# Placing the swapped values in two operations, later zero fills, wider load spacing, and a new written order in a transformer block on one core

## The chip, the cores and the metric

The kernel runs on one core of a Trainium2 chip. The metric is the device time of one execution in microseconds. Three executions of the kernel before took 259.90, 262.45 and 261.12 us; their median is 261.12 us. One more execution was recorded by the hardware profiler and took 260.01 us, of which the span from the first to the last instruction is 258.3 us.

The engines are named as in the profile: PE is the matrix engine, with its weight loads shown apart as PEld, DVE the vector engine, ACT the scalar engine, POOL the GpSimd engine, SP the engine that here only issues DMA transfers.

## The reference

The reference is a block with two halves on x of 2048 tokens by 512 features: sliding-window attention with 32 heads of 16 features, and an MLP that mixes along the tokens (1792 hidden). Shifts, scales and gates come from a small vector c. Cut to what matters:

```python
def _A_ref(x, wqkv, wo):                 # H = 32, Dh = 16, W = 256
    q, k, v = split(x @ wqkv)
    scores = einsum('bhqd,bhkd->bhqk', q, k) * Dh ** -0.5
    mask = (i - j >= 0) & (i - j < W)
    p = softmax(where(mask, scores, -1e9))
    return einsum('bhqk,bhkd->bhqd', p, v).merge_heads() @ wo
def _B_ref(x, w1, b1, w2, b2):           # mixes over the 2048 tokens
    u = gelu(einsum('bsd,sf->bdf', layernorm(x), w1) + b1)
    return (einsum('bdf,fs->bds', u, w2) + b2).transpose(0, 2, 1)
mod = (silu(c) @ w_mod); sa, ca, ga, sb, cb, gb = parts(mod)
x = x + ga * _A_ref(layernorm(x) * (1 + ca) + sa, wqkv, wo)
x = x + gb * _B_ref(layernorm(x) * (1 + cb) + sb, w1, b1, w2, b2)
```

## The kernel before

The 2048 tokens are worked in four groups G = 0 to 3 of 512. Each group passes through a projection stage (layer norm, transpose, keys, queries, values), an attention stage and a closing stage (output projection, two layer norms). The groups overlap: while attention of group G runs, the projection of G+1 and the closing of G-1 fill the gaps. The attention work is cut into 75 pieces, called chunks 0 to 74 (15, 20, 20 and 20 for the four groups). A chunk is one set of score matmuls into two PSUM tiles (`pss`, three banks, a single buffer; `psb`, one bank, two buffers), two exponentials on ACT that write the tile `et`, one multiplication with the mask on DVE, and value matmuls on PE (`po`), which are called AV here. The exponential of the three banks is the longest ACT operation, so its number (chunk number) serves as a clock in what follows.

Below, operations are named as in the code. For the values of groups 1 to 3 there are four token tiles of 128 each, and each tile passes through this chain: `v` (four matmuls on PE, tile `pv`), `ve` (DVE copies `pv` to `vb`), `vx` (SP issues two transfers of 32 KB, lines 938 and 939, which carry the values of the half that lies on the wrong 64 partitions from `vb` to `vs`), `vp` (POOL places the values in `VT`, four copies of 64x256: from `vb`, `vs`, `vb`, `vs`). `vb` and `vs` have two buffers each, so the `ve` of a tile waits for the `vp` of the tile two before. `VT` has three buffers of 128x4096 which are taken in turn by the groups; outside the blocks that `vp` writes they must hold zeros, which POOL's memsets `z` provide at the start (one of 128x4096 for `VT[1]`, four of 128x1024 for `VT[2]`). `kk` on POOL splits a copied key tile `kb` into `KT` with a mask by parity. `xn` on POOL and `xt` on SP (line 838) normalize a token tile and transpose it by DMA for the next group. `w1l` on SP (line 1028) loads the seven pieces of `w1`, 512 KB each, that the partial sums of the MLP need (`p`, from chunk 52 on); they land in memory that the pool of the modulation weights has released.

PE keeps three spare PSUM banks (`od0` to `od2`) for the tiles of k, q, v, the output projection and the unit sums of AV. A bank comes free when its copy or its multiplication has run.

The order is written out by hand in two tables. `ORDER` (line 60) lists the numbers of all 1129 operations; `run_schedule` (line 154) emits them in that order, and `CHOSEN` (line 114) says which engine takes an operation that has a choice. The wrapper `Ordered` (line 227) holds PE, DVE, ACT and POOL to that order, and every instruction that it issues has its line, L235. SP is not wrapped (`dma = nc.sync`, line 220): the queue of SP is laid out by the tile framework when the program is built, so it need not follow `ORDER`. In the built program of the kernel before, SP holds, from the fourth transpose for group 2 on: three loads of w1, the fourth `vx` of group 1, four loads of w1, all four transposes for group 3, and then the first `vx` of group 2.

After the attention stage PE alone sets the pace: partial sums, first MLP layer (`u`, `pu`), and second layer (`py`), until 16 tiles of output have been stored.

Of the kernel before, what the change touches and what calls it, by code (L numbers as in the profile page):

```python
# [17 lines left out]
DH = 16  # L18
# [42 lines left out]
    2, 38, 0, 4, 9, 40, 3, 10, 11, 12, 41, 13, 6, 14, 8, 42, 39, 16, 5, 43, 44, 45, 46, 17, 48, 18, 19, 47, 1, 20,  # L61
    52, 51, 50, 7, 49, 56, 57, 58, 60, 59, 61, 53, 74, 62, 75, 126, 76, 79, 127, 77, 63, 84, 80, 55, 64, 85, 78,
    128, 130, 81, 65, 83, 82, 89, 131, 86, 93, 67, 54, 66, 90, 129, 88, 134, 132, 87, 71, 91, 72, 135, 73, 68, 92,
    69, 94, 70, 136, 138, 95, 97, 139, 98, 264, 96, 110, 99, 140, 265, 142, 111, 143, 101, 100, 106, 266, 112, 144,
    166, 267, 102, 113, 167, 145, 103, 268, 15, 104, 168, 170, 107, 171, 141, 146, 114, 137, 147, 115, 148, 133,
    172, 174, 116, 108, 149, 175, 269, 117, 151, 150, 152, 490, 156, 271, 153, 184, 176, 119, 173, 118, 154, 120,
    272, 185, 121, 491, 273, 157, 155, 270, 122, 158, 105, 188, 169, 186, 27, 124, 189, 28, 274, 492, 161, 29, 275,
    162, 159, 125, 198, 163, 24, 160, 123, 190, 276, 493, 25, 199, 21, 177, 109, 22, 26, 200, 202, 23, 30, 164, 494,
    203, 165, 178, 278, 179, 180, 187, 204, 206, 191, 31, 181, 207, 277, 192, 193, 32, 194, 37, 182, 495, 216, 208,
    279, 183, 201, 217, 280, 209, 286, 281, 287, 195, 220, 218, 282, 283, 288, 221, 284, 36, 289, 291, 219, 285,  # L70
    292, 496, 497, 222, 205, 328, 196, 296, 329, 293, 297, 34, 210, 716, 290, 294, 330, 332, 197, 211, 333, 331,
    212, 223, 301, 302, 499, 298, 213, 336, 334, 35, 306, 295, 299, 214, 33, 337, 307, 215, 717, 500, 224, 225, 308,
    338, 346, 501, 498, 718, 310, 347, 311, 339, 309, 226, 944, 502, 303, 348, 350, 312, 227, 230, 351, 300, 335,
    945, 233, 234, 719, 228, 360, 352, 231, 229, 235, 361, 304, 720, 313, 314, 353, 239, 362, 315, 364, 240, 365,
    232, 236, 504, 340, 241, 366, 368, 305, 237, 369, 242, 946, 317, 341, 243, 342, 370, 238, 378, 316, 343, 318,
    379, 349, 320, 319, 321, 244, 721, 344, 354, 380, 382, 345, 355, 383, 245, 324, 503, 325, 246, 384, 392, 322,
    356, 393, 371, 512, 326, 513, 357, 367, 396, 394, 509, 514, 397, 510, 363, 247, 515, 511, 372, 398, 723, 400,
    947, 381, 505, 358, 248, 401, 506, 249, 385, 373, 725, 374, 359, 327, 402, 410, 507, 517, 375, 323, 411, 395,
    518, 386, 387, 519, 376, 414, 250, 727, 412, 532, 415, 533, 377, 516, 728, 388, 403, 255, 416, 424, 522, 520,
    389, 399, 425, 523, 251, 534, 417, 508, 426, 428, 524, 404, 390, 429, 256, 405, 525, 539, 391, 521, 413, 406,  # L80
    724, 430, 252, 432, 540, 407, 433, 431, 527, 722, 253, 528, 541, 427, 434, 535, 442, 536, 408, 435, 443, 537,
    409, 529, 418, 542, 444, 254, 446, 530, 543, 447, 257, 419, 948, 526, 420, 538, 448, 554, 258, 544, 421, 555,
    449, 436, 726, 437, 545, 259, 438, 556, 445, 558, 546, 439, 557, 422, 547, 559, 423, 729, 450, 451, 548, 440,
    562, 560, 452, 441, 949, 261, 563, 459, 561, 460, 263, 730, 456, 564, 461, 572, 262, 453, 457, 565, 573, 731,
    531, 458, 732, 454, 468, 576, 574, 550, 455, 577, 549, 733, 462, 463, 469, 578, 950, 586, 464, 465, 587, 260,
    466, 470, 551, 467, 588, 590, 553, 735, 591, 471, 736, 552, 566, 472, 737, 592, 594, 567, 589, 595, 579, 738,
    748, 593, 596, 604, 749, 605, 597, 739, 473, 575, 568, 750, 569, 608, 606, 740, 475, 580, 581, 570, 607, 741,
    609, 582, 474, 598, 951, 571, 477, 476, 583, 618, 610, 752, 619, 481, 479, 753, 599, 478, 751, 584, 622, 754,
    620, 600, 585, 623, 755, 482, 743, 734, 756, 480, 624, 626, 744, 611, 601, 627, 483, 742, 745, 628, 636, 484,
    746, 612, 637, 613, 757, 485, 614, 621, 602, 640, 638, 762, 603, 625, 641, 772, 763, 629, 773, 615, 764, 650,  # L90
    642, 774, 488, 651, 765, 759, 760, 643, 486, 630, 639, 616, 761, 654, 487, 652, 631, 655, 632, 653, 644, 489,
    617, 645, 646, 747, 633, 658, 656, 952, 634, 657, 953, 659, 954, 635, 957, 660, 668, 958, 647, 661, 669, 955,
    959, 956, 960, 670, 672, 662, 648, 673, 649, 663, 671, 664, 961, 767, 674, 780, 963, 665, 675, 781, 964, 768,
    965, 782, 769, 784, 966, 666, 770, 785, 667, 676, 783, 677, 967, 678, 786, 788, 685, 679, 787, 789, 686, 682,
    771, 687, 683, 680, 798, 790, 776, 681, 684, 799, 688, 758, 791, 689, 777, 694, 800, 802, 691, 779, 778, 803,
    766, 692, 695, 968, 693, 804, 812, 969, 801, 813, 805, 775, 792, 690, 793, 794, 814, 696, 816, 795, 970, 817,
    697, 974, 971, 698, 975, 818, 972, 820, 796, 976, 821, 815, 973, 806, 819, 807, 797, 808, 822, 830, 809, 977,
    823, 831, 979, 699, 978, 980, 981, 832, 701, 700, 834, 810, 824, 835, 811, 825, 703, 702, 826, 982, 707, 836,
    704, 844, 985, 983, 845, 986, 837, 987, 833, 988, 827, 846, 848, 990, 705, 989, 849, 991, 708, 992, 993, 709,
    850, 852, 828, 838, 853, 829, 839, 994, 840, 1001, 706, 995, 854, 862, 841, 1002, 710, 863, 996, 984, 847, 711,  # L100
    997, 855, 998, 864, 851, 866, 962, 842, 1003, 867, 843, 999, 911, 1000, 912, 868, 876, 908, 913, 877, 714, 909,
    865, 1007, 713, 910, 1004, 878, 880, 712, 856, 1005, 881, 857, 914, 715, 858, 1008, 869, 882, 884, 859, 1012,
    883, 885, 1009, 915, 1013, 1010, 879, 860, 894, 916, 861, 1014, 895, 917, 1018, 1011, 1019, 919, 870, 886, 918,
    871, 896, 898, 1015, 897, 899, 887, 1020, 1021, 1016, 872, 900, 888, 1022, 901, 1030, 1017, 889, 873, 920, 890,
    874, 902, 891, 903, 1006, 875, 892, 904, 893, 1059, 905, 921, 1038, 906, 1073, 907, 1039, 922, 926, 927, 923,
    929, 928, 1031, 930, 932, 1032, 1052, 931, 1023, 925, 1024, 933, 1053, 1045, 924, 934, 1066, 1025, 935, 1046,
    936, 1026, 1074, 937, 1027, 939, 1067, 1047, 1028, 938, 1075, 1060, 1040, 940, 1029, 1033, 1080, 941, 1081, 943,
    1054, 942, 1061, 1082, 1034, 1041, 1035, 1048, 1062, 1042, 1036, 1076, 1049, 1043, 1055, 1087, 1056, 1050, 1068,
    1088, 1063, 1069, 1037, 1089, 1044, 1108, 1057, 1070, 1101, 1064, 1051, 1083, 1058, 1102, 1077, 1071, 1094,
    1095, 1065, 1078, 1084, 1090, 1103, 1085, 1091, 1109, 1096, 1097, 1122, 1098, 1104, 1115, 1105, 1110, 1072,  # L110
    1111, 1086, 1092, 1116, 1079, 1123, 1099, 1112, 1117, 1118, 1106, 1100, 1124, 1093, 1125, 1119, 1113, 1107,
    1120, 1126, 1114, 1127, 1121, 1128,
]
CHOSEN = {
    "ACT": [
        47, 48, 51, 76, 78, 88, 1022, 1027,
    ],
    "DVE": [
        49, 50, 52, 70, 73, 81, 83, 86, 91, 95, 99, 101, 104, 108, 112, 114, 117, 119, 122, 124, 248, 250, 252, 254,
        277, 278, 281, 285, 288, 293, 298, 303, 308, 312, 315, 319, 322, 326, 474, 476, 478, 480, 503, 504, 507, 511,  # L120
        514, 519, 524, 529, 534, 538, 541, 545, 548, 552, 700, 702, 706, 729, 730, 733, 737, 740, 745, 750, 754, 757,
        761, 764, 769, 774, 778, 956, 961, 967, 972, 978, 983, 989, 994, 1000, 1005, 1011, 1016,
    ],
    "POOL": [
        704,
    ],
}
BATCH = True
XT_AFTER = -0.7
W1_AFTER = 2.0  # L130
AV_POS = 0.2
LZ_POS = 0.0
M_POS = -0.5
OT_POS = -1.0
# [59 lines left out]
def kernel(  # L194
# [243 lines left out]
    box = {}  # L438
# [17 lines left out]
    def e_stps(e):  # L456
# [8 lines left out]
            deps=[o3], pos=-20)  # L465
# [142 lines left out]
    def proj0():  # L608
# [3 lines left out]
        def normed(half):  # L612
# [43 lines left out]
            if half == 0:  # L656
# [4 lines left out]
                               deps=[cp[dc // 2], o_fm], pos=base + 1.5) for dc in range(ND)]  # L661
                transposed.setdefault(0, []).append(z)
                zeros[2] = [
                    op("z", "POOL", 0.87, lambda e, n=n: po.memset(VT[2][:, 2 * n : 2 * n + 2, :, :], 0.0), deps=hs[half], pos=base + 3.0)
                    for n in range(4)
                ]
            else:
# [684 lines left out]
```

## Time and profile before

| what | value |
|---|---|
| median of three executions | 261.12 us (259.90 to 262.45) |
| profiled execution | 260.01 us, span 258.3 us, mean granted PE clock 0.993 |
| PE busy, share of the span | 236.3 us, 91% |
| DVE, ACT, POOL busy | 203.2, 179.3, 128.1 us |
| first exponential of chunk 0 | 12.57 us after the start |
| last exponential of chunk 74 begins | 174.35 us |
| last stretch, PE alone | about 176 to 255 us |

The busy shares are averages over stages with different limits. Between 20 and 175 us ACT is the fullest engine; after that ACT has little to do and PE has no gaps. So the time is read in two stretches: how early ACT gets through its exponentials, and how much work is then left for PE.

### The profile page before, as it was taken

The numbers are of one execution on the slowest core, as the hardware profiler recorded it, in microseconds if no ns is written. First come the engines' busy times: TensorE is split into PE (matmuls) and PEld (weight loads), VectorE is DVE, ScalarE is ACT, GpSimd is POOL, SyncE is SP. The second block draws the span as 40 slices with busy tenths as digits, with TensorE's granted clock in tenths as the row PEclk, the third lists the DMA queues.
The fourth block names the chain that finished last, engine by engine and source line by source line (L and its number), as shares of the span: only waits on it lengthen the run. The fifth ranks groups of instructions, "written<-read, shape, count | busy, mean of one in ns | idle before, by whom it ended". The sixth has DMA issues, their size and how long they took to land.

```text
span 258.3 us, 8085 instructions
## 1 busy us (share of the span) xinstructions
PE 236.3 (91%) x3385; PEld 122.0 (47%) x3427; DVE 203.2 (79%) x394; ACT 179.3 (69%) x255; POOL 128.1 (50%) x235
## 2 busy tenths in 40 slices
PE   7878889899895999987999999999999999999994
PEld 2555554444442453444544454446444444444443
DVE  5689999998996999899668889898868764444443
ACT  4499999999996999999999999997237410000000
POOL 8587995975994989787904793810000000000000
PEclk9999999999998899999999999999999999999999
DMA  6998421369923000000020024024999201111111
GB/s 220 328 350 244 38 53 25 61 165 288 182 43 51 13 7 1 3 14 13 15 81 13 4 84 139 28 84 130 374 324 394 84 22 42 46 58 41 41 43 41
DMA packets 41341, 27.02 MB, mean 105 GB/s; under 512 B 11992, under 2 KB 37208, under 8 KB 41304
## 3 DMA queue, kind: packets, MB, share of 16 engines
q1 hardware_dynamic: 41008, 25.97, 35.7%
q8 instruction: 27, 0.44, 0.7%
q10 hardware_dynamic: 296, 0.53, 0.6%
q14 instruction: 10, 0.08, 0.1%
HBM read 22.03 MB, written 2.10 MB: 93 GB/s over the span
## 4 chain that ended last, share of the span: by engine, by line
PE 59%; ACT 18%; DVE 15%; issue 5%; DMA 1%; SPq 0%; DVEq 0%
PE py L235 18%; PE pu L235 17%; ACT et L235 15%; PE pss L235 8%; PE po L235 7%; DVE et L235 4%; PE pa L235 3%; DVE vb L235 2%; DVE h L235 2%; ACT lz L235 2%; PE pk L235 2%; PE pv L235 2%; DVE QT L235 1%; DVE st L235 1%; DVE kb L235 1%
## 5 line engine op out<-in xcount | busy, mean ns | idle before, releaser
L235 ACT ACTIVATE et<-pss 128x1536 bf16<-128x1536 f32 x75 | 110.9, 1478 | 2.5 <-PE psb L235 1.8
L235 PE MATMUL pu<-hb,w1p 128*128 128x512 bf16 x213 | 50.8, 380 | 1.2 <-issue 0.9
L235 DVE TENSOR_TENSOR et<-et,maskt 128x1024 bf16<-128x1024 bf16 (+2 forms) x79 | 47.0, 616 | 5.5 <-ACT et L235 5.4
L235 PE MATMUL py<-guT,w2r 128*128 128x512 bf16 (+1 forms) x234 | 48.5, 366 | 0.7 <-DVE otile L235 0.5
L235 ACT ACTIVATE et<-psb 128x512 bf16<-128x512 f32 x75 | 47.0, 628 | 0.0
L235 PE MATMUL pss<-QT,KT 32*128 32x64 bf16 (+3 forms) x720 | 30.1, 232 | 7.2 <-ACT et L235 5.5
L235 PEld LDWEIGHTS <-w2r 128*128 128x128 bf16 x238 | 23.3, 98 | 26.0 <-issue 0.7
L235 PE MATMUL po<-et,VT 128*32 128x64 bf16 (+3 forms) x960 | 32.3, 235 | 1.8 <-DVE vb L235 0.4
L235 PEld LDWEIGHTS <-w1p 128*128 128x128 bf16 x224 | 20.3, 98 | 25.1 <-issue 2.4
L235 PE MATMUL po<-et,ones_bd 128*32 128x256 bf16 (+3 forms) x624 | 31.5, 269 | 0.0
L235 DVE TENSOR_TENSOR otile<-py,xr 128x512 bf16<-128x512 f32 (+1 forms) x17 | 11.2, 660 | 25.5 <-PE py L235 25.3
L235 PEld LDWEIGHTS <-KT 32*128 32x128 bf16 x960 | 16.4, 93 | 29.0 <-issue 27.0
L235 POOL TENSOR_SCALAR KT<-kb,mask_par 128x512 bf16<-128x512 bf16 (+1 forms) x38 | 26.2, 701 | 7.0 <-DVE kb L235 3.9
L235 PE MATMUL psb<-QT,KT 32*128 32x64 bf16 (+3 forms) x240 | 29.5, 232 | 0.0
L235 PEld LDWEIGHTS <-VT 128*32 128x32 bf16 x960 | 19.0, 96 | 15.4 <-issue 13.1
L235 POOL TENSOR_SCALAR xn<-x,rs,nm 128x512 bf16<-128x512 bf16 x24 | 23.5, 984 | 2.2 <-DVE h L235 1.2
L235 PE MATMUL pk<-h1T,wqkv 128*128 128x256 bf16 (+2 forms) x102 | 20.5, 322 | 3.3 <-DVE vb L235 2.4
L235 DVE BATCH_NORM_STATS2 st<-x 128x6 f32<-128x512 bf16 x32 | 21.7, 684 | 1.5 <-DMA x<-in_A_x_dram 1.3
L235 PEld LDWEIGHTS <-wqkv 128*128 128x128 bf16 x164 | 13.8, 97 | 15.7 <-issue 7.6
L235 PE MATMUL pv<-wqkv,h1T 128*64 128x256 bf16 (+1 forms) x107 | 16.9, 320 | 0.2
L235 PE MATMUL pa<-wod,OT 128*128 128x512 bf16 x58 | 16.0, 380 | 0.5 <-issue 0.3
L235 POOL COPY VT<-vb 64x256 bf16<-64x256 bf16 x24 | 12.8, 535 | 7.1 <-DVE vb L235 6.5
(98 smaller groups left out, 319.1 us busy)
## 6 DMA issues: line engine op xcount, KB each, us to landing
w1p<-in_B_w_dram SPq DMA_DIRECT2D x14, 512.0 KB, 5.0
w2r<-in_B_w_dram SPq DMA_DIRECT2D x14, 512.0 KB, 9.2
x<-in_A_x_dram SPq DMA_DIRECT2D x16, 128.0 KB, 4.8
wmod<-in_w_mod_dram SPq DMA_DIRECT2D x4, 512.0 KB, 8.5
out_dram<-otile SPq DMA_DIRECT2D x15, 128.0 KB, 1.7
wqkv<-in_A_wqkv_dram SPq DMA_DIRECT2D x4, 256.0 KB, 5.1
vs<-vb SPq DMA_DIRECT2D x24, 32.0 KB, 1.9
wmod<-in_w_mod_dram ACTq DMA_DIRECT2D x2, 256.0 KB, 3.9
```

The lines of the kernel that those rows point to most:

```text
L235: ins = call(*args, **kwargs)
```

## The change

`vp` becomes two operations on POOL. `vo` places the two blocks that already lie on the right partitions, and needs only `ve`; `vp` places the two that came through `vs`, and needs `vx` and `vo`. The number of copies and their shapes stay. The four memsets of `VT[2]` no longer stand before the first key splits: in the list of operations they come after the projection of group 0, with a dependency on the first `kk`. The planner's cost of a load `w1l` goes from 1.9 to 2.6 and of a `vx` from 0.85 to 1.05. `ORDER` and `CHOSEN` are new (1141 operations). They move a few operations to other engines: one of the two first copies of transposed x from ACT to DVE, one copy of queries from ACT to DVE, one copy of keys from DVE to ACT, one copy of a partial sum from DVE to ACT, and one pair of multiplications of the closing stage (`m2`) from DVE to POOL.

```diff
-    2, 38, 0, 4, 9, 40, 3, 10, 11, 12, 41, 13, 6, 14, 8, 42, 39, 16, 5, 43, 44, 45, 46, 17, 48, 18, 19, 47, 1, 20,
...
+    39, 2, 3, 38, 9, 40, 1, 10, 11, 4, 12, 41, 13, 14, 42, 16, 8, 43, 44, 45, 17, 46, 18, 48, 47, 19, 6, 20, 7, 51,
...
     "POOL": [
-        704,
+        712, 714,
     ],
...
-                zeros[2] = [
-                    op("z", "POOL", 0.87, lambda e, n=n: po.memset(VT[2][:, 2 * n : 2 * n + 2, :, :], 0.0), deps=hs[half], pos=base + 3.0)
-                    for n in range(4)
-                ]
...
+        zeros[2] = [
+            op("z", "POOL", 0.93, lambda e, n=n: po.memset(VT[2][:, 2 * n : 2 * n + 2, :, :], 0.0), deps=k_done[0, 1][-1:], pos=1.0 + n)
+            for n in range(4)
+        ]
...
-            def e_vp(e):
+            def e_vp(e, own):
                 for half in range(2):
                     rows = slice(KB * half, KB * half + KB)
-                    for block, src in ((half, box["vb", tb][rows, half, :]), (1 - half, box["vs", tb][rows, :])):
-                        po.tensor_copy(
-                            out=VT[r3][rows, 2 * tb + block, :, half * DH : (half + 1) * DH],
-                            in_=src.rearrange("p (a d) -> p a d", d=DH),
-                        )
+                    block, src = (half, box["vb", tb][rows, half, :]) if own else (1 - half, box["vs", tb][rows, :])
+                    po.tensor_copy(
+                        out=VT[r3][rows, 2 * tb + block, :, half * DH : (half + 1) * DH],
+                        in_=src.rearrange("p (a d) -> p a d", d=DH),
+                    )
...
-            vx = op("vx", "SP", 0.85, e_vx, deps=[ve_op], pos=pos)
-            b = op("vp", "POOL", 1.95, e_vp, deps=[vx] + war + zeros[r3], pos=pos)
+            vx = op("vx", "SP", 1.05, e_vx, deps=[ve_op], pos=pos, extra=0.1)
+            own = op("vo", "POOL", 0.97, lambda e: e_vp(e, True), deps=[ve_op] + war + zeros[r3], pos=pos)
+            b = op("vp", "POOL", 0.97, lambda e: e_vp(e, False), deps=[vx, own] + war + zeros[r3], pos=pos)
...
-            loaded.append(op("w1l", "SP", 1.9, lambda e, n=n: load_w1(n, 0), deps=loaded[-1:] or [opened],
+            loaded.append(op("w1l", "SP", 2.6, lambda e, n=n: load_w1(n, 0), deps=loaded[-1:] or [opened],
```

What the built programs hold can be read from their instruction streams. SP's part around groups 1 to 3 (T is a transpose, by its group; the number after vx counts the twelve pairs):

```
before: T1 x4, T2, vx1, T2, vx2, T2, vx3, T2, w1 x3, vx4, w1 x4, T3 x4, vx5, vx6, vx7, vx8, vx9 ...
after:  T1 x4, T2, vx1, T2, T2, T2, vx2, w1 x2, vx3, w1 x5, vx4, T3, vx5, T3, vx6, T3, T3, vx7, vx8, vx9 ...
```

PE's part around the fourth value tile of group 1 (S is the score part of a chunk, AV23 the first AV that reads that tile): before `S23 q k k AV23 S24`, after `S23 AV22 q q AV23 S24`.

## The prediction

> **What bounds the kernel now.** First the page's busy times by slice, to see which engine is full where.
>
> ```profile
> ACT  4499999999996999999999999997237410000000
> POOL 8587995975994989787904793810000000000000
> PEclk9999999999998899999999999999999999999999
> ```
>
> ACT is at 9 from the third slice (13 us) to the 27th, but for one slice: the 13th, 77.5 to 84 us, has 6, and the granted PE clock falls there too. After the 27th slice (174 us) ACT thins out and PE is full. So the end is set by ACT's pace to about 176 us, then by the PE work left, and what ACT loses on the way is carried to the end. The table of stretches of 2 us shows the hole.
>
> ```profile
> 78.00:80.00 2.00, 1.26 (x50) 0.95 (x52) 1.70 (x3) 2.00 (x4) 0.00 (x0) 1.00 0.76 73
> 80.00:82.00 2.00, 0.41 (x24) 0.23 (x13) 0.22 (x1) 1.59 (x2) 1.08 (x3) 1.00 0.23 53
> 82.00:84.00 2.00, 1.12 (x13) 0.35 (x13) 2.00 (x5) 0.00 (x0) 1.89 (x4) 0.60 0.14 37
> ```
>
> The columns after the 2.00 are PE, PEld, DVE, ACT, POOL busy, then clock, DMA share and GB/s. Its cause is read in the timeline, in order of time.
>
> ```profile
> 66.45 11.53 SPq L838 DMA_TRANSPOSE h1T<-xn  x4
> 78.09 1.30 SPq L938 DMA_DIRECT2D vs<-vb  x1
> 80.83 0.39 POOL L235 COPY VT<-vs 64x256 bf16<-64x256 bf16 x1 [3.27 <-DMA vs<-vb]
> 81.78 0.69 DVE L235 CAST vb<-pv 128x512 bf16<-128x512 f32 x1 [2.08 <-POOL VT L235]
> 82.52 0.58 PE L235 MATMUL pk<-h1T,wqkv 128*128 128x512 bf16 x1 [2.11 <-DVE vb L235]
> 84.67 1.45 ACT L235 ACTIVATE et<-pss 128x1536 bf16<-128x1536 f32 x1
> ```
>
> The pair vx5 stood on SP behind four transposes, went out at 78.09 and held up vp on POOL, then the next ve (buffer ring of two), then a PSUM bank, then PE, then chunk 32's exponential. Chunk 31's began at 79.55, so this step took 5.12 us where the seven before it took (79.55 - 64.97) / 7 = 2.08: **the hole costs 3.04 us**. I then looked for the same chain one step away from breaking, where the loads of w1 run.
>
> ```profile
> 53.59 2.36 SPq L1028 DMA_DIRECT2D w1p<-in_B_w_dram  x3
> 56.05 1.76 SPq L938 DMA_DIRECT2D vs<-vb  x1
> 58.49 5.96 SPq L1028 DMA_DIRECT2D w1p<-in_B_w_dram  x4
> 62.89 0.39 POOL L235 COPY VT<-vs 64x256 bf16<-64x256 bf16 x1 [2.66 <-DMA vs<-vb]
> 64.13 0.30 PE L235 MATMUL po<-et,VT 128*32 128x128 bf16 x8
> 64.97 1.47 ACT L235 ACTIVATE et<-pss 128x1536 bf16<-128x1536 f32 x1
> ```
>
> vx4, behind three loads, took 6.8 us to land (median of all pairs 1.9); its copies ended at 64.08 and AV23, which reads them and stands before S24, began at 64.13. It was just in time, with nothing to spare.
>
> **The change part by part.**
>
> *Split.* The copies stay four of 0.40 (medians). In each of POOL's three waits for a pair (9.3 us in all) one copy already ran before the wait; now both own copies do: 0.4 each, on POOL only. I take 0; bounds 0 and -0.4 on the chain of a late pair.
>
> *Zero fills.* Four memsets of 0.95 move behind key splits. The split of the third key tile (16.31) can come 0.95 earlier; chunk 3 then waited for DVE's vb and not for it, so nothing is won. In their new places POOL had idle time (0.83, 0.51, 0.53 between 17.6 and 23.1; the last stands just ahead of the wait for vx4). Without that cover each would cost up to 0.95. I take 0.
>
> *Engine moves and the new start.* A first copy goes from ACT (two in a row, 0.59 each) to DVE, where it delays the scales by as much: 0. The value copy ve is put before the first mask (0.81), while the 0.4 us widening copy of the modulation vector comes between; chunk 3's exponential had idled 0.54 before its `psb`. I take -0.6 at chunk 3, bounds -0.9 and +0.5 (the mask now being late). One m2 pair on POOL costs two of 1.2, under POOL's 4.59 us wait before 162.03; DVE gives up 0.85, not on the chain. 0.
>
> *Wider loads.* The 2.6 is a planner's cost. Nothing in the program holds a load back: its waits are the released memory and the DMA issued eight earlier. In the built program the loads stand back to back, and, after SP's T2, T2, T2, vx2, **the fourth pair stands behind all seven instead of three**. This is the step on which the sum turns:
>
> - First load. xn on POOL: own copies 45.6 to 46.4, xn 47.2, swapped copies 48.1, xn 48.9; transpose to 50.2 (1.22 each), two issues of vx2 to 51.3. So 51.4, 50.8 if the early start is kept, 52.1 if the transposes take 2.3 as one did; before 53.59.
> - Data. Seven loads are 3.67 MB. In the stretches from 58 to 68 us the queue moved 291 GB/s (281 in one), DMA share 1.2, and it was done at about 68.6: 15.0 us after the first issue. So 66.4 here (65.8 to 67.1).
> - Landing. Before, 1.57 MB ahead of vx4 had moved by about 60.5 and it landed at 62.85; an undisturbed pair lands 1.7 to 1.9 after issue. I add 1.6 (0.8 to 2.3): 68.0, range 66.6 to 69.4.
> - Two swapped copies, 0.85: AV23 at 68.9 (67.4 to 70.3) against 64.13. Chunk 24's exponential is late by **4.7 us (3.3 to 6.2)**, less where PE reaches AV23 late for other reasons; I take 4.5. The start's 0.6 is no further gain: the landing sets the time.
>
> Queued behind the waiting vp on POOL are the key split of chunk 25, a statistics chain, and the next xn: all wait. On PE everything behind AV23 waits.
>
> A page speaks for a shorter wait. The Trainium skill, "DMA: Bandwidth & Descriptors", Specifications, gives an HBM limit of about 358 GB/s per core; by it, as an estimate, the 3.67 MB would take 10.2 instead of 12.6 us and the sum would be 2.4 lower. The 291 GB/s of this trace decides.
>
> *The old hole.* In the new queue one transpose, not four, stands before vx5, and two before vx6. After vp at 68.9 POOL has: key split 1.8, statistics 3.5, xn 0.8, xn2 0.9, own copies 0.8, xn 0.8, xn2 0.9, key split 1.8, own copies 0.8, swapped 0.8: 81.8. With everything 4.5 later, the matmuls whose ve needs that buffer end at about 82.5. So the old hole closes, -3.04 (0 if POOL slips by over 1 us).
>
> **Sum:** +4.5 - 3.0 = +1.5 on the profiled 260.01 (span 258.3 and 1.7 around it), 261.5. That run stands 1.1 under the median; on the median the forecast is **262.6**. From chunk 52 on PE is full in both orders with the same work, so it adds nothing.
>
> **Rivals.**
>
> *The fourth pair slips through (faster).* It is issued when the ring takes it: the seven loads' own issues took 8.3 us, vx3's 1.2, so at about 61. Were it to land like an undisturbed pair, 1.9 later, vp would be done by 64 and no new wait arises: -3.0 - 0.6 = 257.5. For it: a small transfer. Against it: the 6.8 us behind only three loads. The Trainium skill, "DMA: Bandwidth & Descriptors", Queues, rings and completion order, says that completion is not FIFO for an issuing engine, though each DMA engine takes its descriptors in ring order. By the first half it would be this rival, by the second the forecast; the 6.8 us agree with the second.
>
> *Both holes (slower).* POOL's list above has 0.7 us to spare. From 82.5 on, each us that POOL is late passes through ve, bank and PE to chunk 32; If it is late by the whole former 3 us, nothing of the old hole is saved: 261.1 + 4.5 = 265.6. For it: single copies of 0.40 have run up to 0.90, and POOL stands at 9, 8, 9 in the three slices after the hole. Against it: each engine behind the new wait starts later too.
>
> *The spacing holds (the change does what it says).* If the loads did start apart, vx4 would land within 2 us: 257.5 as in the first rival. Against it: the built order.
>
> **How the numbers follow.** Forecast 0.55, pair slips through (with the spacing) 0.25, both holes 0.20. One per cent of the median, 2.6 us, is about what a measurement can tell from no change. The forecast's own range, 260.5 to 264.5, lies mostly within; its end above 263.7 holds 0.12 and a tail below 258.5 holds 0.01. The fast cases give 0.23 faster and 0.02 same, the slow one 0.20 slower. So faster 0.24, same 0.44, slower 0.32. The range takes in both rivals and what is a little beyond the second: 257.5 to 266.0.
>
> **What would show it.** In the new profile: seven w1p issues from about 51 us with one pair between; POOL waiting about 6 us for `vs` near 68; AV23 and a 6.5 us step between the exponentials of chunks 23 and 24; a lower PE clock behind it; steps of 2.1 from chunk 31 to 32. Wrong would be: that POOL wait under 3 us, the hole at chunk 32 still there, or loads that start apart. Not seen here, and able to upset the sum, is a wait in the new PE order that no engine of before shows.

## The result and the profile after

The changed kernel takes 270.0 us (median of four runs, 268.86 to 270.37) against 260.51 us of the kernel before on the same chip: ratio **1.0344 [1.0277, 1.0411]** (95% interval in brackets), slower. Slow executions are left out of every ratio, the longest being one of a_three (459.5 us) and one of a_z_pieces (801.83 us). The profiled execution took 270.37 us, its span is 268.6 us, the mean granted clock 0.975 (before: 260.01, 258.3, 0.993). The forecast was 262.6, in a range of 257.5 to 266.0.

The page's slices of the changed kernel, 6.7 us each:

```profile
DVE  5689999998149999999966978899787784454443
ACT  4189999999069999999899999999336630000000
PEclk9999999999569999998899999999999999999999
```

ACT now has a hole of its own in the 11th slice (67 to 74 us), almost empty, with DVE at 1 in the same slice and the clock down to 5 and 6 around it. The 6 behind it is the rest of the same hole; where the old one would now stand, near 92 us, ACT is at 9. The first slices differ too: ACT is at 4, 1, 8 where it was at 4, 4, 9. The list of waits (engine, what it waited for, from whom; us in total, times, longest) names the large ones:

```profile
ACT et L235 <- PE psb L235: 11.2, 8, 7.7
POOL VT L235 <- DMA vs<-vb: 7.9, 1, 7.9
PE po L235 <- POOL VT L235: 7.3, 1, 7.3
ACT h1T L235 <- PE psb L235: 4.1, 1, 4.1
```

The first three are one chain, pair to POOL to PE to ACT. The fourth is at the start. To see where the rest arises I set the starts of the 75 large exponentials of both traces side by side:

| chunk | before | after | later by | what lies between |
|---|---|---|---|---|
| 0 | 12.57 | 15.19 | 2.62 | start |
| 23 | 62.84 | 64.91 | 2.06 | |
| 24 | 64.97 | 74.79 | 9.82 | the wait for the pair |
| 25 | 66.93 | 78.13 | 11.19 | a low clock behind it |
| 31 | 79.55 | 90.94 | 11.40 | |
| 32 | 84.67 | 93.25 | 8.58 | the old hole, closed |
| 47 | 116.68 | 125.25 | 8.58 | |
| 48 | 118.62 | 128.69 | 10.07 | a second loss |
| 74 | 174.35 | 184.76 | 10.40 | |

So four places make the difference, and the path behind chunk 52 adds almost nothing.

**Start.** The timeline of before, then that of after (start, duration, engine, line, operation, idle time before it in brackets):

```profile
2.03 3.52 POOL L235 MEMSET VT<- 128x4096 bf16 x1
5.83 0.75 DVE L235 TENSOR_SCALAR xn<-x,mv,rs 128x512 bf16<-128x512 bf16 x2 [0.56 <-ACT rs L235]
```

```profile
4.57 3.52 POOL L235 MEMSET VT<- 128x4096 bf16 x1
5.47 3.08 DVE L235 TENSOR_SCALAR xn<-x,mv,rs 128x512 bf16<-128x512 bf16 x2 [0.29 <-ACT rs L235]
8.29 0.61 PE L235 MATMUL psb<-identity,xn 128*128 128x128 bf16 x4 [1.83 <-DVE xn L235]
```

The new order puts the building of the masks ahead of the large fill on POOL. DVE begins its first two normalisations earlier than before (5.47), but they last 3.08 us instead of 0.75. The first alone runs from 5.47 to 8.23; the fill ends at 8.08.

**The pair.** The timeline of after around the loads of w1:

```profile
55.81 1.16 SPq L1029 DMA_DIRECT2D w1p<-in_B_w_dram  x2
59.04 8.20 SPq L1029 DMA_DIRECT2D w1p<-in_B_w_dram  x5
67.35 1.65 SPq L938 DMA_DIRECT2D vs<-vb  x1
72.78 0.85 POOL L235 COPY VT<-vs 64x256 bf16<-64x256 bf16 x2 [7.92 <-DMA vs<-vb]
73.69 0.30 PE L235 MATMUL po<-et,VT 128*32 128x128 bf16 x4 [7.34 <-POOL VT L235]
74.79 1.45 ACT L235 ACTIVATE et<-pss 128x1536 bf16<-128x1536 f32 x1 [7.66 <-PE psb L235]
78.13 1.45 ACT L235 ACTIVATE et<-pss 128x1536 bf16<-128x1536 f32 x1 [1.10 <-PE psb L235]
```

The fourth pair goes out behind all seven loads, POOL waits 7.92 us, and chunk 24 comes 9.88 after chunk 23. The next step is long too, 3.34, and stretches of 2 us tell why (length, then PE, PEld, DVE, ACT and POOL busy, clock, DMA share, GB/s):

```profile
70.00:72.00 2.00, 0.00 (x0) 0.00 (x0) 0.00 (x0) 0.00 (x0) 0.00 (x0) 0.50 0.49 131
74.00:76.00 2.00, 2.00 (x56) 1.44 (x56) 0.00 (x0) 1.21 (x1) 1.83 (x6) 0.50 0.04 8
76.00:78.00 2.00, 2.00 (x22) 0.36 (x14) 1.07 (x3) 1.03 (x3) 1.69 (x5) 0.50 0.00 0
```

While all stand still the granted clock falls to 0.50 and stays there for some 4 us of full PE work.

**The old hole.** One transpose, then the pair, then one transpose, and the step to chunk 32 is 2.30:

```profile
79.71 1.20 SPq L838 DMA_TRANSPOSE h1T<-xn  x1
82.05 0.47 SPq L938 DMA_DIRECT2D vs<-vb  x1
84.82 1.20 SPq L838 DMA_TRANSPOSE h1T<-xn  x1
90.94 1.45 ACT L235 ACTIVATE et<-pss 128x1536 bf16<-128x1536 f32 x1
93.25 1.45 ACT L235 ACTIVATE et<-pss 128x1536 bf16<-128x1536 f32 x1
```

**Chunk 48.** In the new PE order the scores of chunks 46 and 47 stand next to each other, and the second must wait for ACT:

```profile
123.00:125.00 2.00, 0.28 (x21) 0.19 (x15) 1.97 (x4) 2.00 (x3) 2.00 (x3) 1.00 0.11 28
125.00:127.00 2.00, 1.75 (x54) 1.00 (x43) 2.00 (x5) 2.00 (x4) 1.94 (x4) 0.79 0.06 12
127.00:129.00 2.00, 2.00 (x27) 0.65 (x29) 1.97 (x5) 0.78 (x2) 0.37 (x1) 0.50 0.00 0
```

PE is busy 0.28 of 2 us, then the clock falls to 0.50, a key projection of four matmuls takes 1.86 instead of the 1.02 of a_two, where the clock stayed up, and chunk 48's exponential is late (step 3.44, before 1.94).

### The profile page after: what moved, and what is told of

The parts are those of the page before. It is cut to its first block, busy times and chain, and to the rows that moved or that the text cites. A ratio compares the mean times of both kernels' runs of the same rounds, so it can differ in the third digit from the quotient of the medians.

```text
span 268.6 us, 8136 instructions
## 1 busy us (share of the span) xinstructions
PE 244.2 (91%) x3427; PEld 122.8 (46%) x3427; DVE 203.8 (76%) x392; ACT 180.0 (67%) x255; POOL 131.4 (49%) x237
## 4 chain that ended last, share of the span: by engine, by line
PE 61%; DVE 14%; ACT 9%; POOL 6%; issue 5%; DMA 3%; SPq 0%; DVEq 0%; ACTq 0%
PE pu L235 19%; PE py L235 18%; PE po L235 8%; ACT et L235 7%; PE pss L235 6%; PE pa L235 3%; DVE et L235 3%; DMA vs<-vb 3%; PE pk L235 3%; POOL VT L235 2%; POOL KT L235 2%; DVE vb L235 2%; PE pq L235 2%; DVE xn L235 2%; DVE st L235 2%
## 5 line engine op out<-in xcount | busy, mean ns | idle before, releaser
L235 PE MATMUL pu<-hb,w1p 128*128 128x512 bf16 x224 | 52.6, 380 | 0.0
L235 DVE TENSOR_TENSOR et<-et,maskt 128x1024 bf16<-128x1024 bf16 (+2 forms) x79 | 48.8, 632 | 2.4 <-ACT et L235 2.2
L235 PE MATMUL po<-et,VT 128*32 128x64 bf16 (+3 forms) x960 | 33.1, 239 | 8.4 <-POOL VT L235 7.3
L235 PE MATMUL po<-et,ones_bd 128*32 128x256 bf16 (+3 forms) x624 | 32.7, 275 | 0.0
L235 POOL TENSOR_SCALAR KT<-kb,mask_par 128x512 bf16<-128x512 bf16 (+1 forms) x38 | 27.4, 731 | 9.5 <-ACT kb L235 8.0
L235 PEld LDWEIGHTS <-KT 32*128 32x128 bf16 x960 | 15.6, 93 | 31.0 <-issue 29.0
L235 DVE TENSOR_TENSOR OT<-po,lz 128x256 bf16<-128x256 f32 x32 | 13.3, 417 | 16.2 <-ACT lz L235 16.1
L235 PE MATMUL pk<-h1T,wqkv 128*128 128x256 bf16 (+2 forms) x108 | 21.7, 331 | 0.8 <-DVE vb L235 0.5
L235 POOL TENSOR_SCALAR xn<-x,rs,nm 128x512 bf16<-128x512 bf16 x24 | 21.6, 903 | 1.4 <-DVE h L235 0.5
L235 PE MATMUL pa<-wod,OT 128*128 128x512 bf16 x64 | 17.0, 380 | 0.6 <-DVE OT L235 0.4
```

The source lines that it names most:

```text
L235: ins = call(*args, **kwargs)
```

## The experiments

The theory at this point: **four separate places**, namely the fill on POOL that holds DVE at the start (+2.6), the pair's place in the queue (+7.8, and +1.4 through the clock), PE's order at chunk 48 (+1.5), and the closed hole (-2.8). Each run changes one place, in the changed kernel (names with a) or in the kernel before (b). Where pairs, transposes and first w1 loads are "kept on SP", their issues were pinned to program order, as the other engines' are; the order is given in the short form of the section on the change. Steps are between the starts of large exponentials. Medians of the kernel before in the four sessions were 262.75, 261.6, 260.06 and 260.93, so ratios are compared.

```diff
+    sp = Ordered(nc.sync)
...
-            dma.dma_start(out=h1T[:, :, i * P : (i + 1) * P], in_=xn[i][:], transpose=True)
+            sp.dma_start(out=h1T[:, :, i * P : (i + 1) * P], in_=xn[i][:], transpose=True)
...
-        dma.dma_start(out=t[:], in_=w1_v[:, 8 * half : 8 * half + 8, 2 * P * pair : 2 * P * (pair + 1)])
+        (dma if half else sp).dma_start(out=t[:], in_=w1_v[:, 8 * half : 8 * half + 8, 2 * P * pair : 2 * P * (pair + 1)])
```

### The start: the fill first again (a_z_first)

```diff
 POOL, changed kernel
-masks, fill 128x4096, kk0 ...
+fill 128x4096, masks, kk0 ...
```

> The changed kernel with one thing put back: on POOL the 3.52 us fill of the second value tile stands ahead of the building of the masks again, as in the kernel before. Theory A (DVE's first normalisation stands still while POOL fills): the two xn take about 0.8 us instead of 3.08, the first large exponential begins at 12.6 us instead of 15.19, the loads of w1 and all behind them move up by as much, and the time is 270.0 - 2.6 = 267.4. Rival B (the start is late because its first copy and scales moved between ACT and DVE, or because x and the modulation weights landed later): xn short or not, the first exponential stays within 0.5 us of 15.2 and the time within 0.5 of 270.0. Rival C (the landing of the fourth pair sets the time however early the start is): first exponential at 12.6, but chunk 24 as late as it was, time 270.0.

Ratio 1.0116 [1.0071, 1.0160]. The median is 265.8, 4.2 us below the 270.0 of the changed kernel; the ratio falls by more, because the kernel before, measured beside it, took 262.75 instead of 260.51. The xn took 0.87 and the first exponential began at 11.25, 3.9 earlier. So A's mechanism is right and its size was too small, and B and C are out. The pair, later in the same trace:

```profile
51.45 1.16 SPq L1029 DMA_DIRECT2D w1p<-in_B_w_dram  x2
68.09 0.85 POOL L235 COPY VT<-vs 64x256 bf16<-64x256 bf16 x2 [7.59 <-DMA vs<-vb]
70.10 1.45 ACT L235 ACTIVATE et<-pss 128x1536 bf16<-128x1536 f32 x1 [7.33 <-PE psb L235]
```

First load, landing and chunk 24 moved up by 4.4 to 4.7, and POOL's wait is nearly as long as it was: early or late, the pair lands some 17 us after the first load.

### The start, in the kernel before (b_masks_first)

```diff
 POOL, kernel before
-fill 128x4096, masks, four fills 128x1024 ...
+masks, fill 128x4096, four fills 128x1024 ...
```

> The kernel before with one part of the change alone: the masks are built on POOL ahead of the 3.52 us fill of the second value tile. Theory A (DVE's first normalisation stands still while POOL fills): the two xn take about 3 us instead of 0.75, the first large exponential begins at about 15 us instead of 12.57, and the time rises by 2.3 to 2.8 to about 263.1. Rival B (the late start comes from the moved copy or from landings): no change, 260.5.

Ratio 1.0123 [1.0070, 1.0176]. The two xn lasted 4.33, and the first exponential began at 16.37, 3.8 later. A again, larger than forecast: the first xn ran from 5.77 to 9.06 and the second to 10.10, because here three fills follow one another on POOL until 9.95. In this trace the fourth pair is late too, with three loads ahead of it as before (POOL waits 4.15 for it, step to chunk 24 5.01), and the old hole is down to a step of 3.00, so the ratio isn't the price of the start alone.

### Does DVE wait for one POOL instruction, or for the work? (a_z_pieces)

```diff
-po.memset(VT[1][:], 0.0)
+[po.memset(VT[1][:, n : n + 1, :, :], 0.0) for n in range(8)]
```

> The changed kernel, order kept, with the one 128x4096 fill of 3.52 us on POOL cut into eight of 128x512. Theory A1 (DVE waits for the end of the single POOL instruction that it meets): the first normalisation is held for at most one piece, some 0.5 us, the two xn take 0.8 to 1.8 us instead of 3.08, and the first large exponential begins between 11.3 and 13.2 us instead of 15.2; ratio to the kernel before 1.012 to 1.024. Rival A2 (DVE and POOL share bandwidth while both work on such data, or POOL has to be through with all its queued fills): the xn still take about 3 us until the last piece ends, first exponential at 14.4 to 15.5, ratio 1.030 to 1.040.

```profile
4.50 4.07 POOL L235 MEMSET VT<- 128x512 bf16 x8
6.14 1.02 DVE L235 TENSOR_SCALAR xn<-x,mv,rs 128x512 bf16<-128x512 bf16 x2 [0.56 <-ACT rs L235]
```

The same bytes are filled at the same time, and the xn take 1.02 instead of 3.08, single ones 0.42 and 0.69, in the middle of pieces of 0.53. First exponential 12.20, ratio 1.0222 [1.0111, 1.0332]. A1 holds: what is waited for is the end of a POOL instruction, not of the whole fill. It need not be the first one that is met: in b_masks_first the first xn (until 9.06) got through only behind the second of three fills (ends 8.03, 8.92 and 9.95).

### The pair's place (a_pin, a_pair5, a_pair4, b_pair4_last)

```diff
 SP, changed kernel; a_pin: its own order, pinned
 a_pair4
-... w1 x2, vx3, w1 x5, vx4, T3, vx5 ...
+... w1 x2, vx3, w1 x1, vx4, w1 x4, T3, vx5 ...
 a_pair5
+... w1 x2, vx3, w1 x3, vx4, w1 x2, T3, vx5 ...
 SP, kernel before; b_pair4_last
-... w1 x3, vx4, w1 x4, T3 x4 ...
+... w1 x7, vx4, T3 x4 ...
```

> The changed kernel with transposes, pairs and first w1 loads kept on SP in exactly the order that they have there: the base for the runs that move the pair. Theory A: as the changed kernel, ratio to the kernel before 1.030 to 1.040, and step from chunk 23 to 24 about 9.9. Rival B (the pin itself, and not the pair's place, made the run with the pair behind three loads fast): step under 5 and ratio under 1.01.

> The changed kernel, SP kept in its order but for the fourth pair of group 1, which stands behind five w1 loads instead of seven (behind three it was just in time, 0.45 us of waiting on POOL). Theory A (the pair lands when the loads ahead of it have moved; 512 KB at the 291 GB/s of the queue are 1.8 us each): the pair lands 3.6 before its time with seven, POOL waits 3.5 to 5 for vs, the step from chunk 23 to 24 is 5 to 7 and the ratio 1.010 to 1.022, about half of the way from 0.992 to 1.034. Rival B (the pair is late only when the queue is full with all seven, or only by its own issue): step under 3 and ratio 0.99 to 1.00, or as with seven.

> The changed kernel with the transposes, pairs and first w1 loads kept on SP in the order that it has, but for one move: the fourth pair of group 1 stands behind three of the seven loads instead of behind all seven. Theory A (the pair's place in the queue is the price): POOL's 7.92 us wait for vs near 72 us shrinks below 3, the step from chunk 23 to 24 falls from 9.88 to 2.1 to 3, the clock behind it stays near 1, and the time is 270.0 less 7.7 to 9.0, so 261.0 to 262.3; the late start of 2.6 and the loss at chunk 48 of 1.4 stay. Rival B (the wait comes from the loads' contention or from the new order of PE and POOL around chunk 24): the step stays above 7 and the time within 1 of 270.0. Rival C (the wait only goes elsewhere): chunk 24 is on time, but the old hole at chunk 32 returns, 264 to 265.

> The kernel before with one part of the change alone: the fourth pair of group 1 stands on SP behind all seven w1 loads instead of behind three; transposes, pairs and loads are otherwise kept in the order they had. Theory A: first load at 53.6, the queue done at 68.6, the pair landed at about 70.2, AV23 at 71.1 instead of 64.13, so chunk 24 late by 7.0, with up to 1.3 more from a lower clock behind it; the old hole at chunk 32 stays. Time 260.5 + 7.0 to 8.3, 267.5 to 268.8. Rival B (the order of the engines around chunk 24 in the changed kernel is needed for it): within 1 of 260.5. Rival C (the new wait swallows the old hole, since both are the same POOL chain): 264 to 266.

| run | loads ahead of the pair | POOL's wait | step 23 to 24 | ratio |
|---|---|---|---|---|
| a_pin | 7 | 7.67 | 9.63 | 1.0296 [1.0229, 1.0362] |
| a_pair5 | 5 | 4.10 | 6.06 | 1.0161 [1.0102, 1.0221] |
| a_pair4 | 3 | 0.45 | 2.09 | 0.9921 [0.9891, 0.9951] |
| b_pair4_last | 7 | 11.22 | 11.97 | 1.0202 [1.0157, 1.0246] |

The pin costs nothing by itself (1.0296, where the changed kernel had 1.0344). From the first load's issue to the copy behind the landing it takes 17.0 us with seven loads ahead (55.81 to 72.78), 13.2 with five (56.43 to 69.58) and 9.5 with three (55.16 to 64.67): 1.9 us for each 512 KB, that is 280 GB/s. The price is the bytes in front, and A holds. The timeline of a_pair4 shows the pair landed with four more loads issued behind it:

```profile
58.30 0.58 SPq L235 DMA_DIRECT2D w1p<-in_B_w_dram  x1
59.05 1.10 SPq L235 DMA_DIRECT2D vs<-vb  x2
60.20 6.14 SPq L235 DMA_DIRECT2D w1p<-in_B_w_dram  x4
64.67 0.86 POOL L235 COPY VT<-vs 64x256 bf16<-64x256 bf16 x2 [0.45 <-DMA vs<-vb]
```

In b_pair4_last the same move makes chunk 24 late by 9.8 and chunk 25 by 1.2 more, but the old hole falls to a step of 2.70 with 2.82 two chunks on, so 1.5 net is given back: rival C holds there in part, and the ratio comes to 5.3 us on that session's 262.75, less than the 7.0 to 8.3 expected.

**The move of a_pair4 alone brings the changed kernel back to the time of the kernel before, or just under it**: the ratio is 0.9921, but the kernel before had its highest median in that session, and the two profiled spans are 258.2 and 258.3.

### The base and the hole (b_pin, b_hole)

```diff
 SP, kernel before; b_pin: its own order, pinned
 b_hole
-... w1 x4, T3 x4, vx5, vx6, vx7 ...
+... w1 x4, T3, vx5, T3, vx6, T3, T3, vx7 ...
```

> The kernel before with transposes, pairs and first w1 loads kept on SP in exactly the order that they have there. It is the base for the runs that move one of them: ratio to the kernel before 0.998 to 1.002, steps between exponentials as in the kernel before. On this chip the kernel before took 262.75 instead of 260.5; if its fourth pair is sometimes late, as the 0.05 us between copy and AV23 allow, the step from chunk 23 to 24 is above 2.5 here.

> The kernel before with one part of the change alone: on SP the first pair of the next group stands behind one transpose and the second behind two, instead of both behind all four; everything else keeps its place. Theory A (that queue order makes the 3.04 us hole at chunk 32): the step from chunk 31 to 32 falls from 5.12 to 2.1 to 2.8 and the ratio to the kernel before is 0.987 to 0.992. Rival B (the hole is POOL's list of work, which is as late without the queue): step above 4, ratio 0.997 to 1.003. Rival C (the transposes, now later, hold up the scaling of h1T and the projections of chunks 40 to 48): the hole closes and 1 us or more is lost behind chunk 36.

b_pin: ratio 0.9988 [0.9945, 1.0031], and in its trace the step to chunk 24 is 4.32. So in the kernel before's own order the fourth pair can be late, by 2 us, where the one trace of the kernel before had 0.05 us of slack. How often the unpinned kernel meets this isn't shown, as no other trace of it was kept. b_hole: ratio 0.9895 [0.9840, 0.9950], step to chunk 32 2.07. A holds: the queue order makes the old hole. Of the 2.8 us that the trace has won by chunk 33, 0.8 are lost again by chunk 47, in four steps of 0.1 to 0.4, as C would have it in small.

### The loads apart, as the schedule writes them (a_written)

```diff
 SP, changed kernel
-T1 x4, T2, vx1, T2, T2, T2, vx2, w1 x2, vx3, w1 x5, vx4, T3, vx5 ...
+T1 x4, vx1, vx2, T2, w1, vx3, T2, vx4, w1, T2, T2, w1, vx5, w1, T3, vx6 ...
```

> The changed kernel with transposes, pairs and first w1 loads kept on SP in the order in which the schedule writes them: the seven loads stand apart, with three pairs and four transposes between the first and the fourth of them, and two and three more operations between those behind. Nothing else is changed. Theory A (the wait at chunk 24 came from the loads standing together in front of the pair, and the spacing was what would have prevented it): the step from chunk 23 to 24 is under 3, POOL's wait for vs under 3, ratio to the kernel before 0.985 to 0.997, about that of the run with the pair alone moved (0.992). Rival B (pinning this order makes transposes wait behind pairs that are not ready, since SP then issues in strict order): waits of 2 us or more on h1T or vs between chunks 15 and 40, ratio above 1.0.

Step to chunk 24 2.09, so the wait is gone, as A has it, but the ratio is 1.0023 [0.9995, 1.0051]. The trace says what is left: the first exponential at 15.15 (fill and xn), and chunk 48 at a step of 3.66 with the clock at 0.53. No wait of B's kind is seen. The spacing that the change speaks of would have worked, had the built program kept it.

### Do the repairs add, and what is chunk 48? (a_three, a_two, a_best)

```diff
 all three: fill first (a_z_first) and pair behind three loads (a_pair4)
 PE, a_two
 ... S46, S47, AV51, AV52, k29, k30, S48 ...
 PE, a_three
+... S46, AV51, S47, AV52, k29, k30, S48 ...
 PE, a_best
+... S46, S47, AV51, AV52, k29, S48, k30 ...
```

> The changed kernel with three repairs together: the 3.52 us fill ahead of the masks on POOL, the fourth pair behind three w1 loads on SP, and on PE one AV (of the unit that stands between the scores of chunks 46 and 47 in the kernel before) moved back between those two scores. If the three losses are separate, as theory A has it, they add: against the run with the pair alone moved (0.992 of the kernel before) the start gives 3.1, since the first exponential there was at 14.4 and with the fill first at 11.3, and chunk 48 gives 0.4 to 1.0; the ratio to the kernel before is 0.976 to 0.981. Rival B (with an earlier start the pair is late again, because the loads start earlier and the landing sets chunk 24): the step from chunk 23 to 24 grows by 2 or more and the ratio stays above 0.985.

> The changed kernel with two repairs: the 3.52 us fill ahead of the masks on POOL, and the fourth pair behind three w1 loads on SP. The run with three repairs showed that the third (an AV between the scores of chunks 46 and 47) did not help: chunks 48 and 49 lost 0.8 and 0.9 there, with the clock at 0.5. Theory A (the loss at chunk 48 comes from PE standing idle before that score and from a clock that drops behind it, and the AV's place is not its cause): start and chunk 24 as in the run with three, chunk 48 late by 0.4 if the clock stays up and by 1.4 if it drops; ratio to the kernel before 0.980 to 0.990. Rival B (the AV did help): chunks 48 and 49 lose over 2.0 here and the ratio is above that of the run with three, 0.9865.

> The run with two repairs and one more: on PE the scores of chunk 48 stand between the two pieces of the key projection that stood ahead of them and waited for a PSUM bank. Theory A (these scores are late because they stand behind both pieces, which wait for the bank that DVE's OT frees): the exponential of chunk 48 comes 0.4 earlier than in the run with two repairs if the clock stays up there, and up to 1.4 if it drops; ratio 0.977 to 0.988, no more than 0.005 below the run with two. Rival B (what is late is the bank, and moving the scores only hands the delay to the key copies and so to chunk 56 and on): chunk 48 is early, but chunk 52 and on stand where they stood.

Ratios 0.9865 [0.9793, 0.9938], 0.9880 [0.9828, 0.9932] and 0.9862 [0.9816, 0.9907]: the second repair adds to the first in the traces (chunk 74 at 174.23 with the pair alone, at 170.44 with both), though the intervals of the two ratios overlap (0.9921 and 0.9880, in two sessions). The run with three missed the 0.976 to 0.981 expected of it, and the third repair in either form is worth nothing that can be measured. With two, the steps to chunks 48 and 49 are 2.39 and 2.33 (1.94 and 2.13 before); with the scores moved they are 2.09 and 2.63, the same sum: the delay is the key projection's wait for a bank, and is handed on, as rival B had it. With the AV moved they are 2.71 and 3.02, with the clock at 0.50.

The larger part of that loss is the clock, and it isn't the same in every execution. All ten profiles with the changed kernel's PE order have PE busy 0.37 to 0.43 us in the 2 us behind chunk 46's exponential (0.83 with the AV moved). Behind it the clock fell to between 0.50 and 0.57 in six of them (the changed kernel, a_z_first, a_z_pieces, a_three, a_written, a_pin) and stayed at 1.00 in four (a_pair4, a_pair5, a_two, a_best). Where it stayed, chunks 48 and 49 lose 0.65 together, where it fell 1.4 to 1.8. The Trainium skill, "TensorE: Matmul & The Clock Gate", Part 1, says that the clock is set by activity in a window of 4096 cycles that runs freely and doesn't start with the kernel. By that rule the same idle time can fall inside one window or be cut in two, which could make the six and the four; no run here tests it.

### The two parts that the change names (b_vtpart, b_split, b_all)

```diff
 b_split, POOL: in each placing
-own, swapped, own, swapped
+own, own, swapped, swapped
 b_vtpart: b_split, and
-fill 128x4096, masks, four fills 128x1024, kk0 ...
+fill 128x4096, masks, kk0, fill, kk2, fill, vp0, fill, ..., fourth fill before vo2 of the second group
 b_all: b_vtpart, and SP as in b_hole
```

> The kernel before with the two parts of the change that its words name, and no order but theirs: each placing of values in two operations, both copies of own values and then both of swapped ones, and the four fills of the third value tile behind key splits and ahead of the first value copies of the second group. Theory A (both cost and gain nothing): ratio 0.997 to 1.003, steps as in the kernel before; at the pair of chunk 24 one own copy of 0.4 less stands behind the wait. Rival B (the fills delay POOL's first work of the second group, which has no time to spare): a later AV23 and 1 to 2 us more, ratio 1.004 to 1.008. Rival C (the own copy ahead of the wait takes the pair's 0.4 off chunk 24 whenever it is late): ratio 0.995 to 0.998.

> The kernel before with the split alone: both copies of own values, then both of swapped ones; the fills where they were. Theory A (the split is what gained in the run with split and fills: behind a late landing two copies of 0.4 stand before the values are ready, and not three): the hole at chunk 32 shrinks from a step of 5.1 to 5.4 to one of 2.7 to 4.7, where chunk 24 is late it is late by 0.4 less, ratio 0.992 to 0.997. Rival B (it was the fills): ratio 0.998 to 1.003.

> The kernel before with split, moved fills, and on SP the first two pairs of the next group behind one and two transposes instead of four; the engines' orders are those of the kernel before. Theory A (split and queue order work on the same hole, so they add only in part; at chunk 24 the split takes away the occasional lateness): the step from chunk 31 to 32 is 2.1 to 2.8, chunk 24 on time, ratio 0.982 to 0.989. Rival B (they add in full): 0.9895 x 0.9935, that is 0.983 or lower. Rival C (no gain over the queue order alone): 0.989 to 0.992.

b_vtpart gains: 0.9935 [0.9903, 0.9967]. b_split doesn't: 0.9999 [0.9966, 1.0032]. So the gain comes with the fills (no run moves them without the split), and the start shows it, first in the kernel before, then in b_split, then in b_vtpart:

```profile
8.07 1.92 POOL L235 MEMSET VT<- 128x1024 bf16 x2
8.66 1.47 DVE L235 TENSOR_SCALAR h1T<-h1T,modFM 128x256 bf16<-128x256 bf16 x3
```

```profile
7.94 1.98 POOL L235 MEMSET VT<- 128x1024 bf16 x2
8.00 2.00 DVE L235 TENSOR_SCALAR h1T<-h1T,modFM 128x256 bf16<-128x256 bf16 x3
12.44 1.45 ACT L235 ACTIVATE et<-pss 128x1536 bf16<-128x1536 f32 x1
```

```profile
7.67 0.86 DVE L235 TENSOR_SCALAR h1T<-h1T,modFM 128x256 bf16<-128x256 bf16 x3
10.97 1.45 ACT L235 ACTIVATE et<-pss 128x1536 bf16<-128x1536 f32 x1
12.06 0.95 POOL L235 MEMSET VT<- 128x1024 bf16 x1
```

It is the same collision: the scales of h1T run into two of the small fills and take 1.47 in the kernel before and 2.00 in b_split, instead of 0.86. What it costs depends on how they meet: in b_pair4_last, with the fills where they were, the scales met one fill only (1.38) and the first exponential began at 11.53. Of the 3.2 us between the traces of b_split and b_vtpart at chunk 74, 1.5 come from the start. The other 1.8 come from the old hole: chunks 31 to 34 take 8.05 instead of 9.89, and why the hole is smaller no run tests. Rival B of b_vtpart, that the fills delay POOL, is out.

b_all has a ratio of **0.9785 [0.9741, 0.9829]**, 255.82 us where the kernel before took 260.93, and beats both kernels. That is below theory A's 0.982 to 0.989 and as rival B had it: the two gains add in full. The step to chunk 32 is 2.22; there is still 1.1 to be had at chunk 34 (step 3.20). It has the kernel before's orders on all engines but SP, and the fills moved. Its span is 254.5; that of a_best, with the changed kernel's orders, is 254.1, and their first exponentials are as far apart (11.30 and 10.81). By ratio b_all is the better one (0.9785 against 0.9862, in two sessions). So **the new orders of PE, ACT and DVE have shown no gain of their own**, once fill and pair are put right; whether they cost anything these runs don't settle.

## Why the prediction was wrong

The place of the large loss and the closed hole were right, and 262.6 was not, because of steps ahead of and behind them.

- **"Engine moves and the new start", -0.6 (-0.9 to +0.5): the step that failed.** Measured +2.6 at chunk 0 and +2.3 at chunk 3, where the forecast had it; it reaches the sum through the first load, below. That POOL's large fill moves behind the masks was not priced, since POOL had time and nothing waits for that fill. DVE had no semaphore to wait for, but an operation of 0.4 stood for 2.76. Without it (a_z_first) the first exponential begins at 11.25 and that of chunk 3 at 17.66, 2.0 before the kernel before, better than the forecast.
- **"Zero fills ... nothing is won", 0 (cost up to 0.95 each): wrong in sign.** I looked for what waits for POOL, and not for what runs on DVE while POOL fills. The row was in the trace of before, 1.47 for three operations of 0.34 beside 1.92 of fills. Moving the fills is worth 0.2 to 1.7 at the first exponential (10.97 and 11.30, against 11.53 in b_pair4_last and 12.44 to 12.63 in the kernel before, b_split, b_pin and b_hole), and with the split 0.65% of the time.
- **Split, 0: right** (0.9999).
- **First load 51.4: failed too.** It was issued at 55.81, 4.4 later. The first load moves as the start does: 2.1 earlier for a start 2.3 earlier at chunk 23 (a_z_first), 2.2 later for one 2.1 later (the changed kernel). The forecast's 51.4 stood on the start as it was before, and for that start the runs put the load near 53.6. So half of the 4.4 is the late start, and half is the work that stands ahead of the loads. From the first own copy to the end of the last xn POOL took 4.9 us (48.30 to 53.21, as long in a_z_first), where the forecast had 3.3 (45.6 to 48.9): it took 0.8 each for the own copies and the last xn, and they lasted 1.39 and 1.49. What stretched them no run tests.

```profile
48.30 1.39 POOL L235 COPY VT<-vb 64x256 bf16<-64x256 bf16 x2
51.72 1.49 POOL L235 TENSOR_SCALAR xn<-x,rs,nm 128x512 bf16<-128x512 bf16 x1
```

- **From first load to landing, 16.6 us: right.** That a_z_first has 51.45, 68.09 and 69.00 where the forecast had 51.4, 68.0 and 68.9 is luck, two errors that cancel: an early load in the forecast and an early start in the run. What was right in itself is the time from first load to landing (16.6 there, 16.9 in the changed kernel) and the queue's rate.
- **"Took 4.5" for the whole wait: mis-sized.** The low clock was named as a sign and not priced; it cost 1.4 at the next chunk, here and in a_z_first alike.
- **Old hole -3.04: right**, measured -2.8. Chunks 31 to 32 took 2.30, forecast 2.1.
- **"A wait in the new PE order" was named as able to upset the sum, without a price.** It came at chunk 48: 0.65 by the bank, and about 0.9 more where the clock fell.
- **No change from chunk 52 on: right**, +0.3.
- **The rivals.** "The pair slips through" is out: the wait grows by 1.9 us with each load ahead. "Both holes" didn't come. "The spacing holds" would have removed the wait (a_written), but the built order didn't hold it, as forecast. The lower sum by the Trainium skill's HBM limit of about 358 GB/s per core ("DMA: Bandwidth & Descriptors", Specifications) is out as well: this queue moved 280.

The sum by the traces, from chunk to chunk: +2.1 (start, by chunk 23), +7.8 (pair), +1.4 and +0.2 (clock and drift), -2.8 (hole), +1.5 (chunk 48), +0.3: 10.4, where the spans differ by 10.3. The forecast's +1.5 lacked 5.3 by chunk 24, of which 4.4 are the later first load, 1.6 of clock and drift, 0.2 of the hole, 1.5 at chunk 48 and 0.3 behind. The run with the start alone put right (a_z_first) took 265.8, or 263.5 if its ratio is put on 260.51: inside the range, though from a start that was better than the forecast's.

## What to carry to other kernels

When an operation is moved on POOL, look at what DVE does in that time, even if no semaphore joins the two: here a long fill on POOL held the normalisations and scales that it overlapped on DVE until it ended, so cut long fills up or put them where DVE waits for something else. A small transfer that is needed soon landed here when the bytes ahead of it in the queue had moved, so its place is priced in bytes; and a schedule's spacing counts only if the built queue keeps it. A wait that empties PE is to be priced with the slower clock behind it.

## What the runs showed of the hardware

- **DVE held by POOL.** bf16 normalisations and scales on DVE ended 0.08 to 0.15 us after the end of a POOL fill that they met (8.23 against 8.08 in the changed kernel; 8.97 against 8.89 in b_split), and with fills of 0.53 none lasted over 0.69. Where they met only the last 0.2 us of the large fill, they ended 0.40 after it (5.40 to 5.95 in a_z_first, fill until 5.55). The statistics on DVE kept their 0.67 to 0.69 us inside the 3.52 us fill (before at 2.90, a_z_first at 2.88 and 3.90), and a copy out of PSUM kept its 0.39 inside another fill (b_pair4_last, 13.05 to 13.45, fill 12.56 to 13.51). The Trainium skill, "SBUF — State Buffer", SBUF: two separate sides, states it: VectorE in a two-port mode and GpSimd share a port pair that is locked for the whole instruction, and the loser blocks fully. These traces agree, the unhindered statistics too, if they don't run in such a mode, which no trace shows.
- **The clock** after 1.6 us of idle PE in 2 (1.2 in a_three) fell in six executions and not in four, with nearly the same instructions around it. The longest idle stretch of PE ahead of the fall was 1.7 us. After the long wait for the pair it was at 0.50 to 0.53 from 68 to 78 us, 4 of them of full work.
